# Attention of the first batch by groups of 192 tokens over all heads, in row and column halves of the array

## The chip, the cores and the metric

One Trainium2 chip, one of its cores. The time is microseconds from start to end of one execution on the device, several executions per kernel. Engines are named as in the profile: PE is TensorE's matmuls, PEld its weight loads, DVE VectorE, ACT ScalarE, POOL GpSimd, SP SyncE.

The kernel before has two levels of time, which matter throughout. All its 43 executions, over all experiments, lie either at 314.4 to 316.1 us (15 of them) or at 319.3 to 323.7 (28), with none between. "High level" and "low level" are only names, for times of the kernel before near 320 and near 315 us.

## The reference

Sliding-window attention (batch 8, 8 heads, 576 tokens, head size 64, window 64), then an expert layer on all 4608 tokens.

```python
scores = scale * q @ k.T                      # (8, 8, 576, 576)
mask = (rel >= 0) & (rel < 64)
attn = softmax(where(mask, scores, -1e9))     # divided by sum + 1e-9
x = (attn @ v).transpose(0, 2, 1, 3).reshape(4608, 512)
h = x @ w_in                                  # 512 -> 2048
out = (h * sigmoid(h)) @ w_out                # 2048 -> 512
```

## The kernel before

The kernel describes its work as operations with prices in microseconds, simulates them once when it is built, and emits each engine's instructions in the order that comes out. On the chip that order is fixed; only semaphores say when.

The expert layers run over nine tiles of 512 tokens, first layer (512 to 2048) and then second. TensorE does these products almost without a gap, and the attention of the next batches is woven between them. Nothing can be woven into the start: the first tile needs the attention of batch 0. In the kernel before this goes by pairs of heads, each over all 576 tokens in three groups:

```python
def values(op, n, b, pj, g):                  # per (pair of heads, group of 192 tokens)
    for x in range(3):
        s = 2 * pj * NB + 3 * g + x
        nc.tensor.matmul(at_pv(op)[:, x], lhsT=es[n % NE][:, x].rearrange("p h i -> p (h i)"),
            rhs=vv[b % NK][:, s:s + NB + 1:NB, 0:D + 1], start=(x == 0), stop=(x == 2))
def inverse(op, n):                           # tokens in partitions: 6 sums per partition
    nc.vector.reciprocal(out=rcs[n % NRC], in_=at_pv(op)[:, :, :, D])
# ... the product with the reciprocal, broadcast along the free dimension, as 128x384,
# ... then back_both(): six transposes to features in partitions, and a copy into the bridge
```

The values carry a column of ones, so the 65th column of each output is the sum of exponentials. Tokens lie in partitions, so there are only six sums in each partition: the reciprocal is 128x6. The price is that the output has to be turned for the expert layer.

Two buffers hold the values of two batches; VectorE makes a copy shifted by 64 tokens after each load.

The softmax here doesn't subtract the row's maximum and nothing guards it: scores larger than these inputs give would overflow.

Of the kernel before, what the change touches and what calls it, by code (L numbers as in the profile page):

```python
# [14 lines left out]
class Plan:  # L15
# [12 lines left out]
    def add(self, cls, us, fn, deps=(), lat=0.08, gate=None, dma=None, pool=None, table=None, b=0):  # L28
        if b > 1 and cls in ("cast", "lift", "spread", "mask", "norm"):
            lat = 0.2  # L30
        op = dict(us=us, first=self.rank[cls] + b if b or cls not in self.rank0 else self.rank0[cls], fn=fn, deps=[d for d in deps if d is not None], lat=lat, gate=gate, dma=dma,
                  pool=pool, table=table, seen=None, n=self.count, until=[], bank=None)
        self.count += 1
        self.queues.setdefault(cls, []).append(op)
        return op
# [11 lines left out]
    def run(self):  # L47
# [7 lines left out]
        while left:  # L55
# [6 lines left out]
            while moved:  # L62
                moved = False
                for e in engines:
# [3 lines left out]
                    for c in can[e]:  # L68
# [8 lines left out]
                        if op["pool"] and not any(self.done(self.banks[i]) for i in self.pools[op["pool"]]):  # L77
                            continue
# [4 lines left out]
                    if op["pool"]:  # L83
                        banks = self.banks
                        op["bank"] = min((i for i in self.pools[op["pool"]] if self.done(banks[i])),
                                         key=lambda i: max([u["seen"] for u in banks[i]], default=0.0))
                        banks[op["bank"]] = op["until"]
# [24 lines left out]
def kernel(ctx, tc, q, k, v, w_in, w_out, out):  # L112
    nc = tc.nc
# [15 lines left out]
    PARTS = {0: [(0, 192), (192, TT)]}  # L129
    NXQ, NXK, NXO = 4, 2, 3  # L130
    NRAW, NOX, NRC = 2, 2, 12
    NIV, NPM = 2, 1
# [18 lines left out]
    natbs = [keep.tile([NR, 2 * NM * D], BF16, name=f"natb{i}") for i in range(NNB)]  # L151
# [3 lines left out]
    es = [keep.tile([128, 3, 2, 64], BF16, name=f"e{i}") for i in range(NE)]  # L155
    rcs = [keep.tile([128, 3, 2], FP32, name=f"rc{i}") for i in range(NRC)]
# [5 lines left out]
    bridge = keep.tile([128, B * NB, NDC, 64], BF16, name="bridge")  # L162
# [7 lines left out]
        rank=dict(prime=-8, one=-9, first=-9, dma=-1, ld0=-1, ld1=-1, st=-2, xo=-1.5, xk=-1.4, silu=-3, out=-2, pv=0, ot=0, s=1, moe=99, warm=200, turn=2,  # L170
                  norm=0, inverse=0, bridge=0, exp=1, mask=1, lift=2, spread=2, shift=2, cast=4, late=5, clear=9),
        rank0=dict(turn=-6, cast=-6, lift=-5, shift=-4.5, exp=-4, mask=-4, inverse=-3.5, norm=-3, bridge=-3.2),
        ahead=dict(s=-5.5, exp=-4.6, pv=-5.5, inverse=-4.3, norm=-4.2, ot=-5.5, bridge=-4.25),
# [32 lines left out]
    def clear_vv(i):  # L206
        nc.vector.memset(vv[i][:, :, D:D + 1], 1.0)
        nc.vector.memset(vv[i][0:64, 0, 0:D], 0.0)

    def clear_k(i):  # L210
        nc.vector.memset(kt[i][:, 0:64].bitcast(FP32), 0.0)
# [7 lines left out]

    c_ident = p.add("one", {"POOL": 1.3}, const_ident)  # L220
# [3 lines left out]
    c_q = {i: [p.add("first", {"ACT": 1.0}, lambda e, i=i, hh=hh: clear_q(i, hh), [c_zero]) for hh in range(2)]  # L224
# [7 lines left out]

    def load_cast(w, b, pj, kk):

        nc.gpsimd.dma_start(  # L235
            out=natbs[w].rearrange("p (h y) -> p h y", h=2),
            in_=(q, k)[kk][b, 2 * pj:2 * pj + 2].rearrange("h (p m) d -> p h (m d)", m=NM),
        )

    def load_first(i, kk):  # L240
        nc.sync.dma_start(
            out=nats[i].rearrange("p j m x -> p (j m x)").bitcast(FP32).rearrange("p (h y) -> p h y", h=2),
            in_=(q, k)[kk][0, 0:2].rearrange("h (p m) d -> p h (m d)", m=NM),
        )

    def cast_first(e, i, w):
        copies[e](out=natbs[w], in_=nats[i].rearrange("p j m x -> p (j m x)").bitcast(FP32))

# [44 lines left out]
    def turn_heads(op, w, hs):  # L293

        pst = at_bf16(op).rearrange("x (m p) -> x m p", m=NM)
        heads = natbs[w].rearrange("p (h m d) -> p h m d", h=2, m=NM)
# [57 lines left out]
    def scores_idle(op, b, pj, g):  # L354

        nc.tensor.matmul(
            banks[op["bank"]][:, 0:384], lhsT=ident,
            rhs=(bias0 if g == 0 else bias).rearrange("k x h i -> k (x h i)"), start=True, stop=False)
        for x in range(3):
            t = 3 * g + x  # L360
            nc.tensor.matmul(
                at_sp(op)[:, x], lhsT=kt[b % NK][:, pj * S + t * 64:pj * S + t * 64 + 128],
                rhs=qbd[b % NK][:, pj, :, t * 64:t * 64 + 64], start=False, stop=(x == 2),
            )

# [32 lines left out]
    def ox0(n):  # L398
        return oxs[n // NP % NOX][:, :, n % NP]

# [5 lines left out]
    def normal_both(e, op, n):  # L406

        pv, rc, ob = at_pv(op), rcs[n % NRC], ox0(n)
        if e == "DVE":
            nc.vector.tensor_mul(ob.rearrange("k x (h d) -> k x h d", h=2), pv[:, :, :, 0:D],  # L410
                                 rc.unsqueeze(3).to_broadcast([128, 3, 2, D]))
            return
        for x in range(3):
            nc.scalar.mul(ob[:, x].rearrange("k (h d) -> k h d", h=2), pv[:, x, :, 0:D], rc[:, x, 0:1])

    def back_both(op, n):
        for x in range(3):
            for hh in range(2):
                r = slice(64 * hh, 64 * hh + 64)
                nc.tensor.matmul(banks[op["bank"]][r, 64 * x:64 * x + 64], lhsT=ox0(n)[:, x, r],  # L420
                                 rhs=ident[:, r], start=(x == 0), stop=(x == 2))

    def turn_o(n, b, g):
        n0, i = b * NB + 3 * g, n // NP
# [9 lines left out]
    def to_bridge(e, op, b, pj, g):  # L434
        n0 = b * NB + 3 * g
# [3 lines left out]
    def first_layer(bank, j, ft, c, lo, hi):  # L439
        nc.tensor.matmul(  # L440
            banks[bank["bank"]][:, lo:hi], lhsT=w_in_sb[:, c, ft * 128:(ft + 1) * 128],
            rhs=bridge[:, (j * TT + lo) // 64:(j * TT + hi) // 64, c], start=(c == 0), stop=(c == NDC - 1),
# [26 lines left out]
    exps = {}  # L469

# [13 lines left out]
    def add_batch_qk(b):  # L484
        pool = "at" if b else "all"
        slot, parts = {}, {0: [], 1: []}
        for pj in range(NP):
            kq_done[(b, pj)] = []
            busy = s_last.get((b - NK, pj), []) + ([c_k[b % NK]] if b < NK else [])
            for kk in range(2):  # L490
# [29 lines left out]
                if (b, pj) == (0, 0):  # L520
                    i = n_nat[0] % NN
                    n_nat[0] += 1
                    ld = p.add("ld0", {"SP": 0.45 if kk else 1.2}, lambda _, i=i, kk=kk: load_first(i, kk), dma=1.15)
                    ca = [p.add("cast", {"ACT": 0.84, "DVE": 0.56}, lambda e, i=i, w=w: cast_first(e, i, w), [ld], b=b)]
                    nat_free[i] = ca[0]
                else:
                    ca = [p.add("dma", {"POOL": 0.66}, lambda _, w=w, pj=pj, kk=kk: load_cast(w, b, pj, kk),
                                [natb_free.get(w)], dma=0.55 if b else 0.75)]
# [3 lines left out]
                for hs in ([(0,), (1,)] if b == 0 and not kk else [(0, 1)]):  # L532
                    twos = b > 0 and not kk
# [33 lines left out]

    def add_batch_attention(b):
        pv_last[b], o_rows = [], []
        pool = "at" if b else "all"  # L570
        for g, pj in [(g, pj) for pj in range(NP) for g in range(NG)] if b < NPM else [(g, pj) for g in range(NG) for pj in range(NP)]:
                n = len(g_pv)

                ahead = "0" if b == 0 and g == 0 else ""
                if b == 0:
                    pool = "at" if pj >= 2 and g else "all"
                s = p.add("s" + ahead, {"PE": 0.17 if b else 0.4}, None,
                          kq_done[(b, pj)] + g_pv[n - NE:n - NE + 1] * (n >= NE) + ([] if b else c_bias) + c_q.get(b, []),
                          lat=0.1, gate=scores_may_run, pool=pool, b=b)
                s["fn"] = lambda _, s=s, pj=pj, g=g: (scores if b else scores_idle)(s, b, pj, g)  # L580
                s_last[(b, pj)] = [s]
                ex = p.add("exp" + ahead, {"ACT": 0.5}, lambda _, s=s, n=n: expo(s, n), [s], table="exp", b=b)
                s["until"] = [ex]
                exps.setdefault(b, []).append(ex)
                ma = ex
                if b:
                    ma = p.add("mask", {"DVE": 0.37}, lambda _, n=n, g=g: masking(n, g), [ex, *c_mask], b=b)
                pv = p.add("pv" + ahead, {"PE": 0.17}, None,
# [4 lines left out]
                rc = p.add("inverse" + ahead, {"DVE": 0.21}, lambda _, pv=pv, n=n: inverse(pv, n), [pv] + ([c_ob[n % NOB]] if b else [])  # L593
                           + g_norm[n - NRC:n - NRC + 1] * (n >= NRC), b=b)
                by = {"DVE": 0.37}
                if b >= NXO or (b, g) == (NXO - 1, NG - 1):
                    no = [p.add("norm" + ahead, by, lambda e, pv=pv, n=n, hh=hh: normal_rows(pv, n, hh),
# [4 lines left out]
                    if pj == NP - 1:  # L602
                        xo[n // NP] = [p.add("xo", {"SP": 1.4}, lambda _, n=n, g=g: turn_o(n, b, g), o_rows, dma=1.6)]
# [4 lines left out]
                if b == 0:  # L608
                    no = [p.add("norm" + ahead, {"DVE": 0.56, "ACT": 0.9} if ahead or pj < 2 else {"DVE": 0.56}, lambda e, pv=pv, n=n: normal_both(e, pv, n),
                                [rc] + g_back[n - NP * NOX:n - NP * NOX + 1] * (n >= NP * NOX))] * 2  # L610
                else:
                    no = [p.add("norm" + ahead, by, lambda e, pv=pv, n=n, hh=hh: normal(e, pv, n, hh), [rc], b=b)
                          for hh in range(2)]
                g_norm.append(no[1])
                pv["until"] = no
                ot = p.add("ot" + ahead, {"PE": 0.1 if b else 0.25}, None, no + [c_twoi], lat=0.1, pool=pool, b=b)
# [119 lines left out]
```

## Time and profile before

| | before |
|---|---|
| time, first four runs | 315.95, 319.32, 321.06, 321.66 us |
| span of the profiled run (high level) | 318.8 us |
| first layer starts | 22.1 us |
| second layer starts | 41.9 us |
| longest wait of PE behind a mask | 4.0 us, at 182 us |

The starts are read from the products that use each weight. The columns are line, engine, operation, out<-in, count, then least, median and greatest duration in ns, then the first and last start in microseconds.

```profile
L440 PE MATMUL mp<-bridge,w_in_sb x640: 243/379/382, 22.1 to 301.4; 128*128 128x512 bf16 x128, 128*128 128x192 bf16 x16, 128*128 128x320 bf16 x16
```

Two rows of the groups by form (line, engine, operation, names, shapes, count, then busy us, mean ns of one, then idle time before):

```profile
L381 DVE RECIPROCAL rc<-at 128x6 f32<-128x6 f32 x91 | 17.5, 194 | 10.1 <-PE at L375 8.0 <-ACT ot L455 0.3
...
L410 DVE TENSOR_TENSOR ox<-at,rc 128x384 bf16<-128x384 f32 x6 | 3.2, 541 | 0.1
```

Last, the wait behind a mask that the table names (PE's line, what it waited for, total us, times, longest us):

```profile
PE at L375 <- DVE e L370: 4.0, 1, 4.0
```

### The profile page before, as it was taken

To read this page: it belongs to the slowest core of one execution; us is meant where nothing else is said; L and a number is where in the kernel's file an instruction comes from. 1 tells how busy PE (TensorE), PEld (TensorE's weight loads), DVE (VectorE), ACT (ScalarE), POOL (GpSimd) and SP (SyncE) were. 2 spreads that over 40 slices of the span, in tenths; PEclk is the share of its full clock that TensorE was granted. 3 is DMA by queue.
4 is the path that set the end of the run, shared out by engine and by line. 5 is a ranking of instruction groups with operands and counts; after the bars stand their busy time and mean duration, and the time that the engine had idled before them with its cause. 6 is when DMAs were issued, how large, how long until landed. Compare 5 with 4: busy or idle time off the path is not lost.

```text
span 318.8 us, 6010 instructions
## 1 busy us (share of the span) xinstructions
PE 307.9 (97%) x2198; PEld 168.4 (53%) x2223; DVE 154.5 (48%) x467; ACT 193.4 (61%) x374; POOL 119.2 (37%) x159
## 2 busy tenths in 40 slices
PE   8999999999999999999999869999999999999996
PEld 4778666545664556445544445446544444444444
DVE  4894748934799898923990159606920000000000
ACT  8898786889776565568356721668166126415611
POOL 8947859496829777564454000000000000000000
PEclk9999999999999999999999979999999999999999
DMA  9999999999999999999999933400340020020012
GB/s 144 164 196 186 193 195 161 127 243 129 187 165 135 176 154 152 163 163 163 154 191 175 142 64 90 84 0 36 80 93 2 35 97 0 2 99 33 2 61 70
DMA packets 138108, 37.51 MB, mean 118 GB/s; under 512 B 122464, under 2 KB 133600, under 8 KB 138080
## 3 DMA queue, kind: packets, MB, share of 16 engines
q0 software_dynamic: 95712, 18.06, 74.4%
q1 hardware_dynamic: 42368, 19.08, 33.6%
q8 instruction: 17, 0.28, 0.4%
q14 instruction: 11, 0.09, 0.1%
HBM read 36.70 MB, written 9.44 MB: 145 GB/s over the span
## 4 chain that ended last, share of the span: by engine, by line
PE 85%; DVE 6%; DMA 4%; issue 2%; ACT 1%; POOL 1%; DVEq 0%; POOLq 0%; ACTq 0%
PE mp L449 36%; PE mp L440 32%; PE at L375 5%; PE at L349 4%; DMA vv<-in_v_dram 4%; DVE qbd L314 2%; PE at L680 1%; PE mp L680 1%; DVE ox L404 1%; POOL vv L272 1%; DVE qbd L268 1%; DVE vv L337 1%; DVE vv L335 1%; PE at L308 1%; PE at L420 1%
## 5 line engine op out<-in xcount | busy, mean ns | idle before, releaser
L449 PE MATMUL mp<-w_out_sb,g 128*128 128x512 bf16 (+2 forms) x583 | 141.6, 369 | 1.0
L440 PE MATMUL mp<-bridge,w_in_sb 128*128 128x512 bf16 (+2 forms) x640 | 130.7, 358 | 0.7 <-ACT g L446 0.6
L446 ACT ACTIVATE g<-mp 128x512 bf16<-128x512 f32 (+2 forms) x160 | 86.3, 556 | 29.8 <-PE mp L440 29.3
L440 PEld LDWEIGHTS <-w_in_sb 128*128 128x128 bf16 x640 | 60.1, 98 | 60.3 <-issue 1.4
L449 PEld LDWEIGHTS <-g 128*128 128x128 bf16 x608 | 55.0, 98 | 42.7
L455 ACT COPY ot<-mp 128x512 f32<-128x512 f32 (+2 forms) x34 | 19.0, 561 | 72.1 <-PE mp L449 62.7
L404 DVE TENSOR_TENSOR ox<-at,rc 64x192 bf16<-64x192 f32 x128 | 45.2, 353 | 2.5
L254 POOL DMA_DIRECT2D nat<-in_k_dram x48 | 36.4, 761 | 24.3 <-DMA nat<-in_k_dram 13.0
L367 ACT ACTIVATE e<-at 128x384 bf16<-128x384 f32 x90 | 38.8, 497 | 10.6 <-PE at L349 9.8
L370 DVE TENSOR_TENSOR e<-e,mask 128x384 bf16<-128x384 bf16 x84 | 26.6, 350 | 33.6 <-ACT e L367 32.8
L272 POOL DMA_DIRECT2D vv<-in_v_dram x32 | 32.3, 1014 | 13.1 <-PE at L375 7.2
L375 PE MATMUL at<-vv,e 128*128 128x130 bf16 x273 | 29.8, 220 | 4.1 <-DVE e L370 4.0
L375 PEld LDWEIGHTS <-e 128*128 128x128 bf16 x288 | 22.5, 97 | 20.0 <-DVE e L370 7.6
L254 POOL DMA_DIRECT2D nat<-in_q_dram x32 | 23.4, 735 | 8.1 <-DMA nat<-in_q_dram 4.6
L349 PEld LDWEIGHTS <-kt 128*128 128x128 bf16 x252 | 18.6, 100 | 10.0 <-issue 2.8
L349 PE MATMUL at<-qbd,kt 128*128 128x128 bf16 x252 | 23.6, 222 | 0.3
L381 DVE RECIPROCAL rc<-at 128x6 f32<-128x6 f32 x91 | 17.5, 194 | 10.1 <-PE at L375 8.0
L314 DVE COPY qbd<-at 64x288 bf16<-64x288 bf16 x26 | 12.5, 480 | 11.1 <-ACT qbd L314 7.6
L387 DVE TENSOR_TENSOR ob<-at,rc 64x192 bf16<-64x192 f32 x40 | 14.0, 350 | 0.8
L314 ACT COPY qbd<-at 64x288 bf16<-64x288 bf16 x22 | 10.5, 476 | 2.8 <-DVE qbd L314 2.5
L268 DVE COPY qbd<-raw 64x1152 bf16<-64x1152 bf16 x16 | 8.1, 505 | 8.4 <-DMA raw<-nat 8.0
L235 POOL DMA_DIRECT2D natb<-in_q_dram x15 | 10.0, 665 | 4.9 <-PE at L375 1.4
(69 smaller groups left out, 158.0 us busy)
## 6 DMA issues: line engine op xcount, KB each, us to landing
out_dram<-ot SPq DMA_DIRECT2D x35, 256.0 KB, 2.4
vv<-in_v_dram POOLq DMA_DIRECT2D x32, 144.0 KB, 7.3
nat<-in_k_dram POOLq DMA_DIRECT2D x48, 72.0 KB, 7.9
nat<-in_q_dram POOLq DMA_DIRECT2D x32, 72.0 KB, 7.6
natb<-in_q_dram POOLq DMA_DIRECT2D x15, 144.0 KB, 6.4
w_in_sb<-in_moe_w_in_dram POOLq DMA_DIRECT2D x8, 256.0 KB, 8.7
w_out_sb<-in_moe_w_out_dram POOLq DMA_DIRECT2D x8, 256.0 KB, 7.8
natb<-in_k_dram POOLq DMA_DIRECT2D x7, 144.0 KB, 5.9
```

The source lines that it names most:

```text
L254: nc.gpsimd.dma_start(out=rows(i)[:, pj % 2, :, 64 * hh:64 * hh + 64], in_=(q, k)[kk][b, 2 * pj + hh].rearrange("(m p) d -> p m d", p=NR),)
L272: queue[e].dma_start(out=vv[b % NK][:, 2 * g0 + 1:2 * g1 + 1:2, 0:D], in_=v[b].rearrange("h s d -> (h s) d").rearrange("(g p) d -> p g d", ...
L314: copies[e](out=qbd[b % NK][64 * hh:64 * hh + 64, pj, hh].rearrange("x (p m) -> x p m", m=NM)[:, :, r::2], in_=at_bf16(op)[64 * r:64 * r + ...
L349: nc.tensor.matmul(at_sp(op)[:, x], lhsT=kt[b % NK][:, pj * S + t * 64:pj * S + t * 64 + 128], rhs=qbd[b % NK][:, pj, :, t * 64:t * 64 + 6 ...
L367: nc.scalar.activation(out=es[n % NE], in_=at_sp(op), func=ACTF.Exp, scale=scale)
L370: nc.vector.tensor_mul(es[n % NE], es[n % NE], mask0 if g == 0 else mask)
L375: nc.tensor.matmul(at_pv(op)[:, x], lhsT=es[n % NE][:, x].rearrange("p h i -> p (h i)"), rhs=vv[b % NK][:, s:s + NB + 1:NB, 0:D + 1], star ...
L404: nc.vector.tensor_mul(ox(n)[:, :, r], pv[r, :, hh, 0:D], rc[r, :, hh:hh + 1].to_broadcast([64, 3, 64]))
L440: nc.tensor.matmul(banks[bank["bank"]][:, lo:hi], lhsT=w_in_sb[:, c, ft * 128:(ft + 1) * 128], rhs=bridge[:, (j * TT + lo) // 64:(j * TT + ...
L446: nc.scalar.activation(out=gts[gt][:, lo:hi], in_=banks[bank["bank"]][:, lo:hi], func=ACTF.Silu)
L449: nc.tensor.matmul(banks[bank["bank"]][:, 0:hi - lo], lhsT=gts[gt][:, m * 128:(m + 1) * 128], rhs=w_out_sb[:, f, lo:hi], start=(f == 0), s ...
L455: copies[e](out=ots[ot][:, lo:hi], in_=banks[bank["bank"]][:, 0:hi - lo])
```

## The change

The intent: start the expert layers sooner. Batch 0 is loaded and attended to by groups of 192 tokens over all eight heads. Scores use row halves of the array (head size 64 is the contraction); values and sums use column halves, with v as weights, so that the output comes out with features in partitions and needs no turning. The sums now lie along the free dimension, and matmuls with ones repeat them over 64 partitions. A ring of 48 blocks in place of 72 for the bridge makes room. The first tile is no longer cut into 192 and 320 tokens. The core of the diff:

```diff
-    PARTS = {0: [(0, 192), (192, TT)]}
+    PARTS = {}
+    NBR = 48
...
+    ones = keep.tile([128, 64], BF16, name="ones")
+    sums = [keep.tile([128, 384], FP32, name=f"sum{i}") for i in range(2)]
...
+    for kk in range(2):
+        loads0[(0, kk)] = p.add("start", {"POOL": 0.66}, lambda _, kk=kk: load_group(kk, 0, kk), dma=1.1)
...
+    def values_columns(op, n, c, g):
+        for x in range(3):
+            for j in range(2):
+                for hh in range(2):
+                    nc.tensor.matmul(
+                        at_six(op["bank"])[64 * hh:64 * hh + 64, x, j],
+                        lhsT=vv[0][:, (4 * c + 2 * j + hh) * NB + 3 * g + x, 0:D], rhs=es[n + hh][:, x, j],
+                        start=(x == j == 0), stop=(x == 2 and j == 1))
+        for hh in range(2):
+            nc.tensor.matmul(banks[op["bank2"]][64 * hh:64 * hh + 64, 0:384], lhsT=ones,
+                             rhs=es[n + hh].rearrange("k x h i -> k (x h i)"), start=True, stop=True)
+
+    def inverse_columns(op, n):
+        nc.vector.reciprocal(out=sums[n // 2 % 2], in_=banks[op["bank2"]][:, 0:384])
+
+    def normal_columns(op, n, c, g):
+        nc.vector.tensor_mul(bridge[:, 3 * g:3 * g + 3, 2 * c:2 * c + 2], at_six(op["bank"]),
+                             sums[n // 2 % 2].rearrange("k (x j i) -> k x j i", x=3, j=2))
...
+                rc = p.add("inverse0", {"DVE": 0.53}, lambda _, pv=pv, n=n: inverse_columns(pv, n),
+                           [pv] + (g_norm[n - 4:n - 3] if n >= 4 else []))
```

(The line numbers of the profiles after differ: the first layer is L498, the second L507, the reciprocal L327, its product L330.)

## The prediction

> **What bounds the kernel now.** I read the page's table of engines and its slices first, then busy time by stretch, then the chain of waits, then the rows of single instructions.
>
> ```profile
> PE 307.9 (97%) x2198; PEld 168.4 (53%) x2223; DVE 154.5 (48%) x467; ACT 193.4 (61%) x374; POOL 119.2 (37%) x159
> ...
> PE   8999999999999999999999869999999999999996
> ...
> DMA  9999999999999999999999933400340020020012
> ```
>
> TensorE is busy 97% of the span, and the DMA engines are occupied from about 2 to 184 us. That 97% flatters: before the first expert layer starts, TensorE runs fillers and small matmuls. So I cut the run where the first layer begins, at 22.1 us, and where the second begins, at 41.9 us.
>
> ```profile
> 0.00:22.10 22.10, 20.37 (x267) 13.59 (x268) 15.20 (x53) 19.90 (x39) 18.35 (x31) 1.00 1.34 166
> 22.10:40.00 17.90, 17.30 (x219) 13.13 (x217) 12.00 (x29) 14.46 (x40) 13.50 (x19) 1.00 1.55 190
> ```
>
> The columns are stretch, length, then busy time of PE, PEld, DVE, ACT and POOL, granted clock, DMA share and GB/s. The last counts the bytes as written (bf16): 166 GB/s over 22.1 us is 3.67 MB, while q, k and v of batch 0 are 3 x 4608/8 x 512 x 2 B = 1.77 MB and each of the two weights 2.10 MB. Up to 22.1 us ACT is 90% busy and DVE 69%; in the last six microseconds of it both are over 90%. The front is the attention of batch 0, and everything after it is a queue of matmuls. The first layer waits for all exponentials of batch 0 and for the outputs of the first 192 tokens, so some attention is left over and is woven into it:
>
> ```profile
> 22.28 0.66 PE mp L440 x8
> 22.94 0.21 PE at L420 x6
> 23.16 0.60 PE mp L440 x6
> ...
> 37.77 0.48 ACT qbd L314
> 38.27 0.44 ACT g L446
> 38.71 0.53 ACT kt L327
> 39.24 0.35 ACT g L446
> ```
>
> (Chain of waits: start, length, what.) The L420 pieces are six transposes back of one (pair of heads, group), 0.21 us each. At 38.3 and 39.2 us the chain leaves TensorE: SiLU stands behind the copies of batch 1's q and k on ACT. The other hole that matters lies far from the change:
>
> ```profile
> 171.67 12.93 DMA vv<-in_v_dram
> 184.59 0.03 issue
> ...
> 185.69 0.24 DVE e L370
> 185.94 0.05 issue
> 185.99 0.51 PE at L375 x3
> ```
>
> Batch 7's values need 12.9 us to land. VectorE's fixed order holds their shift ahead of a mask of batch 6, so TensorE sits idle 4.0 us. The stretch 185 to 190 us then has a granted clock of 0.66.
>
> **What the skill says, and whether this trace agrees.** (1) "TensorEngine Tiling (Array Packing)", Theoretical Speedup and Instruction Overhead: a contraction or output width of at most 64 allows up to two tiles at once, but a matmul costs about 60 cycles however few its columns. Before has no row halves to test. Its column halves agree that little is gained at small width: twelve transposes of 96 columns into halves take 0.38 us where six full ones take 0.23 us (the pieces of 0.38 and about 0.23 us in the chain). (2) "VectorE: DVE Perf Modes", Why PSUM operands drop a tier: fp32 from PSUM runs at one element per cycle. The trace agrees: a 128x384 product from PSUM takes 541 ns. (3) "DMA: Bandwidth & Descriptors", Why small descriptors are slow: a fixed cost per piece. The trace agrees: from 4 to 10 us, with v in 256 B reads, 142 GB/s are written; from 40 to 45 us, mostly weights, 206. (4) "TensorE: Matmul & The Clock Gate", What's actually happening: the clock rises after about 3.4 us of activity. The first fillers are about twice as long as later ones, and the clock of 0.66 after the 4.0 us hole agrees too.
>
> **The change, part by part.**
>
> Loads. The first q and k lose the fast path from SP (288 KB as fp32, landed 3.4 to 3.7 us after issue) and their two ACT casts of 0.83 us. Instead, three groups of 192 tokens, all heads, come through GpSimd: 196 KB each of q and k, in 512 B reads where before had 1536 B, and v in 256 B reads as before. Total bytes stay 1.77 MB. At the 142 GB/s of the 4 to 10 us stretch that is 12.5 us. First bytes at about 2.3 us (the first queue in before takes until 1.7 us, and GpSimd spends some 0.8 us on issuing) put the last v at about 14.8, and the last k, which 197 KB of v follow, at 13.4. Completion adds about 1.5 (estimate from v landing at least 3.7 us after the start of an issue of 1.0 us that moves 147 KB). So k of group 2 is usable at about 14.9, v at 16.3.
>
> From k to the last output. Sixteen transposes 0.55. The lift of k, 768 columns: ACT took 0.634 for 576, so 0.83, with the semaphore 0.95. Scores of the first half: two biases 0.16 each, twelve matmuls of 64 columns at no more than 0.04 to 0.05, 0.85 at most, 0.95 with the semaphore. Four exponentials at 0.50 on ACT, 2.0, the second scores hidden beneath them. Values of the second half: twelve small matmuls and two sums of 384 columns, 0.75, with its wait 0.85. Reciprocal 128x384 at one element per cycle, 0.59; product 0.54; semaphores 0.15. Sum 6.6: the first layer may start at 14.9 + 6.6 = 21.5 us, against 22.1. Groups 0 and 1 lie beneath the loads: k of group 1 lands some four microseconds before k of group 2, about what one group costs ACT (four exponentials and its lifts, 3.5 us).
>
> What goes after the start. The first tile is no longer split into 192 and 320 columns. The split pieces ran at about 0.086 us (29 in 2.50) and 0.149 (12 in 1.79), at best about 0.14 for the second: 64 x 0.226 = 14.5 us; 64 of 512 columns at 0.216 are 13.8. Saved 0.7. The leftover L420 groups, six of 0.21, save 1.3; the last leftover values product 0.2. From the first to the second layer before took 19.8 us; after, 13.8 + 2.5 for batch 1's transposes (four times 0.38 + 0.23) + 0.7 for twelve scores = 17.0, plus 0.5 if half of the ACT holes remain. So the second layer starts at 39.0, which would be 2.9 earlier.
>
> But it needs w_out. In the order of issue before the first quarter megabyte of w_out lie 1.77 + 2.10 + 1.77 MB, then 0.26: 1.77 by 14.8 us, the other 4.13 at 187 to 190 GB/s in 22 us, so 37 to 38.5 with completion. That is just early enough. I take 0.4 off for meeting it: 2.5 us.
>
> The ring moves no work: it cuts the bridge from 72 to 48 blocks to make room. Its first wait has batch 5 wait for tile 0, over 50 us old by then. Free.
>
> **The rivals.** *A: the front becomes a wait for DMA.* If 256 B writes of q and k cost like v, 120 GB/s, the loads end 2.3 us later and the first layer starts at about 23.5. The savings after it still stand, so about 318.8. For it: everything now comes through one queue. Against: 512 B reads lie between the two kinds.
> *B: the head start is eaten later.* The DMA engines are full to 184 us, and values of batch 7 set a hole of 4 us. If those loads are bound by DMA and not by released buffers, TensorE merely waits longer: 319. For: GpSimd waits mostly for landings between 142 and 165 us. Against: the chain leads from products of batch 5 through VectorE to the issue of these loads, with 1.1 us of waiting for VectorE last, so it moves along with compute.
> *C: the reordering closes the hole.* All orders are recomputed from estimates, so the shift of v may fall behind the masks: 4.0 + about 1.5 of slow clock off, 311 to 312. Equally a new hole of this kind may open: 321 to 323.
> *D: the first batch stalls inside.* TensorE's order is fixed, so one late load of v holds everything behind it: 2 to 3 us, about 320.
>
> **Range and chances.** 319.3 - 2.5 = 316.8. I lean slightly back for A and B (weight about 0.35 together, 2 us) and slightly forward for C (weight about 0.2, 5 us): 317.0. The three runs of before spread over 5.7 us, which a hole of varying length would explain. The range is 311.5 to 321.5. Faster by over 2% means below 312.9; only C with the whole head start gets there: 0.16. Slower means above 325.7, needing A or D and a new hole: 0.07. The rest, 0.77, is within 2%.
>
> **What would show each step right or wrong.** The first L440-type matmul at 20 to 23.5 us, all exponentials and products of batch 0 before it, and none of the transposes back after it. Last k landing near 15 us, the four last exponentials in a row on ACT, then reciprocal near 0.6 us. The second layer at 39 to 40 us. A DMA rate below 130 GB/s up to 15 us shows A; a longer wait for v of batch 7 with an earlier first layer shows B; none shows C; TensorE idle before values of batch 0 shows D. I am wrong if the first layer starts after 25 us, or if the head start is there at 42 us but not at the end.

## More of the kernel before

The loads of v are another part that matters later.

The load is priced at 1.53 us of transfer a quarter; the shift has a price of its own.

```python
p.add("dma", {"POOL": 1.0}, lambda e, part=part: load_v(e, b, part), busy, dma=1.53)
...
sh = [p.add("shift", {"DVE": 0.1 + 0.18 * (z - a)}, lambda _, hf=hf, a=a, z=z: shift_v(b, hf, a, z), lv[a:z], b=b) for hf in range(2)]
```

## The result, and the profile after

| | before | after |
|---|---|---|
| median | 320.19 us (315.95 to 321.66) | 331.23 us (330.05 to 332.77) |
| span of the profiled run | 318.8 us | 329.9 us |
| first product of the first layer | 22.1 us | 32.5 us, in full flow from 34.96 |
| second layer starts | 41.9 us | 52.0 us |
| wait behind the mask of batch 6 | 4.0 us | 5.3 us |

The change is slower: ratio 1.0438, interval 1.0347 to 1.0528. Below I compare levels and starts, and give ratios only beside them.

The first views of the kernel after, the table of engines and the slices, in the same columns as before:

```profile
PE 308.3 (93%) x2150; PEld 161.3 (49%) x2175; DVE 165.8 (50%) x453; ACT 184.1 (56%) x337; POOL 120.5 (37%) x161
...
PE   5876799999999999999999939999999999999995
...
PEclk9969999999999999999999998999999999999999
```

PE's busy time is the same as before (308.3 against 307.9 us); its share fell. The holes are in the first five of forty slices, and the granted clock dips there. Two stretches of that time:

```profile
22.10:40.00 17.90, 13.25 (x116) 6.06 (x115) 12.39 (x11) 7.24 (x14) 13.55 (x18) 0.89 1.58 190
...
14.00:34.90 20.90, 12.92 (x189) 6.51 (x182) 20.35 (x19) 7.23 (x14) 15.57 (x21) 0.84 1.62 188
```

In the second, from 14.0 to 34.9 us, VectorE (the third number) is busy for 20.35 of 20.90 us with only 19 instructions, while ACT idles for two thirds. More than a microsecond an instruction: a few are very long. The chain of waits names them:

```profile
14.04 2.56 DVE sum L327
...
16.62 0.56 DVE bridge L330
17.18 2.47 DVE sum L327
...
21.44 2.47 DVE sum L327
...
25.46 2.48 DVE sum L327
...
28.63 2.57 DVE sum L327
...
31.22 0.56 DVE bridge L330
31.78 2.47 DVE sum L327
...
34.35 0.57 DVE bridge L330
...
34.96 4.91 PE mp L498 x22
```

All six reciprocals lie on the chain: from 14.04 us on they are 15.0 of 20.9 us, their products 2.3, and the rest is mostly VectorE's shifts of v and a copy of q. The same line's instructions, and the first starts of the layers:

```profile
L327 DVE RECIPROCAL sum<-at x4: 2546/2546/2547, 17.1 to 31.7; 128x384 f32<-128x384 f32 x4
```
```profile
L507 PE MATMUL mp<-w_out_sb,g x25: 377/379/379, 52.0 to 60.0; 128*128 128x512 bf16 x25
```

The reciprocal takes 2.55 us where the prediction had 0.59 and the kernel's own schedule 0.53. Its product, 0.557, is as predicted (0.54). From the full flow of the first layer to the second it is 52.0 - 34.96 = 17.1 us; predicted were 17.5, and before took 19.8. So the savings after the start are there. The start was lost.

The loads of the last group, from GpSimd's timeline (start, length, what, and in brackets the idle time before it and what ended it):

```profile
1.30 0.91 POOL L247 DMA_DIRECT2D natb<-in_q_dram  x1 [0.85 <-POOLq L811]
...
9.88 0.84 POOL L247 DMA_DIRECT2D natb<-in_k_dram  x1
...
17.13 2.23 POOL L368 DMA_DIRECT2D w_in_sb<-in_moe_w_in_dram  x3 [0.27 <-DMA natb<-in_k_dram]
```

The third k is issued at 9.9 us and its transfer ends at 16.9 (GpSimd, which waits for it, goes on at 17.1); predicted were 14.9. This is a second, smaller miss. Last, the wait behind the mask is still there (L448 is that mask):

```profile
PE at L453 <- DVE e L448: 5.3, 1, 5.3
```

### The profile page after: what moved, and what is told of

Its sections match the earlier page's. It is cut to its first block, busy times and chain, and to the rows that moved or that the text cites. A ratio compares the mean times of both kernels' runs of the same rounds, so it can differ in the third digit from the quotient of the medians. Undisturbed runs are those within 1.5% of the kernel's fastest.

```text
span 329.9 us, 5840 instructions
## 1 busy us (share of the span) xinstructions
PE 308.3 (93%) x2150; PEld 161.3 (49%) x2175; DVE 165.8 (50%) x453; ACT 184.1 (56%) x337; POOL 120.5 (37%) x161
## 4 chain that ended last, share of the span: by engine, by line
PE 87%; DVE 6%; DMA 3%; issue 2%; POOL 1%; ACT 0%; DVEq 0%; POOLq 0%; ACTq 0%
PE mp L507 36%; PE mp L498 36%; PE at L453 5%; DVE sum L327 5%; PE at L439 4%; DMA vv<-in_v_dram 3%; PE at L773 1%; PE at L398 1%; PE mp L773 1%; DVE bridge L330 1%; PE at L489 1%; POOL vv L362 0%; DVE vv L289 0%; PE at L389 0%; POOL natb L247 0%
## 5 line engine op out<-in xcount | busy, mean ns | idle before, releaser
L507 PE MATMUL mp<-w_out_sb,g 128*128 128x512 bf16 (+2 forms) x583 | 141.7, 369 | 1.0
L498 PE MATMUL mp<-bridge,w_in_sb 128*128 128x512 bf16 x576 | 130.1, 379 | 1.9 <-DVE bridge L330 1.9
L504 ACT ACTIVATE g<-mp 128x512 bf16<-128x512 f32 x144 | 84.3, 597 | 37.8 <-PE mp L498 37.3
L498 PEld LDWEIGHTS <-w_in_sb 128*128 128x128 bf16 x576 | 55.3, 98 | 64.8 <-issue 2.2
L507 PEld LDWEIGHTS <-g 128*128 128x128 bf16 x608 | 54.8, 98 | 42.1
L445 ACT ACTIVATE e<-at 128x384 bf16<-128x384 f32 x84 | 35.8, 497 | 11.5 <-PE at L439 11.0
L448 DVE TENSOR_TENSOR e<-e,mask 128x384 bf16<-128x384 bf16 x84 | 27.7, 350 | 28.0 <-ACT e L445 26.8
L362 POOL DMA_DIRECT2D vv<-in_v_dram x28 | 28.4, 1019 | 25.7 <-PE at L453 17.4
L453 PE MATMUL at<-vv,e 128*128 128x130 bf16 x252 | 27.5, 220 | 5.4 <-DVE e L448 5.3
L453 PEld LDWEIGHTS <-e 128*128 128x128 bf16 x252 | 20.2, 97 | 21.8 <-DVE e L448 9.9
L404 DVE COPY qbd<-at 64x288 bf16<-64x288 bf16 x23 | 11.0, 480 | 13.6 <-PE at L398 7.0
L404 ACT COPY qbd<-at 64x288 bf16<-64x288 bf16 x25 | 11.9, 476 | 2.3 <-DVE qbd L404 1.9
L773 PE MATMUL at<-ident 128*128 128x384 bf16 x22 | 7.1, 415 | 3.9 <-POOL ident L189 3.6
```

The source lines that it names most:

```text
L362: queue[e].dma_start(out=vv[b % NK][:, 2 * g0 + 1:2 * g1 + 1:2, 0:D], in_=v[b].rearrange("h s d -> (h s) d").rearrange("(g p) d -> p g d", ...
L404: copies[e](out=qbd[b % NK][64 * hh:64 * hh + 64, pj, hh].rearrange("x (p m) -> x p m", m=NM)[:, :, r::2], in_=at_bf16(op)[64 * r:64 * r + ...
L445: nc.scalar.activation(out=es[n % NE], in_=at_sp(op), func=ACTF.Exp, scale=scale)
L448: nc.vector.tensor_mul(es[n % NE], es[n % NE], mask0 if g == 0 else mask)
L498: nc.tensor.matmul(banks[bank["bank"]][:, lo:hi], lhsT=w_in_sb[:, c, ft * 128:(ft + 1) * 128], rhs=bridge[:, j * TB % NBR + lo // 64:j * T ...
L504: nc.scalar.activation(out=gts[gt][:, lo:hi], in_=banks[bank["bank"]][:, lo:hi], func=ACTF.Silu)
```

## The experiments

Three questions: do the six reciprocals set the loss; what are the two levels; and does the restructured front gain anything in itself?

**e1: copies in place of reciprocals.** The result is wrong; nothing else changes, as the schedule's price stays.

```diff
-        nc.vector.reciprocal(out=sums[n // 2 % 2], in_=banks[op["bank2"]][:, 0:384])
+        nc.vector.tensor_copy(out=sums[n // 2 % 2], in_=banks[op["bank2"]][:, 0:384])
```

> The changed kernel with its six 128x384 reciprocals replaced by copies of the same shape (the result is wrong on purpose; no order changes, since the schedule had priced the reciprocal at 0.53 us anyway). Theory R (the reciprocals, 2.55 us each and back to back on VectorE, delay the first layer): the copy takes about 0.55 us, the first layer starts at 23 to 25 us instead of 35.0, the second at 40 to 42 instead of 52, and the time is 317 to 321 us, the ratio to before 0.99 to 1.01. Rival L (loads through one queue land late, and TensorE's fixed order holds up what follows): the first layer still starts after 28 us and the time stays above 325.

Measured: 321.97 us (320.43 to 322.37), all four runs at the level with the wait (4.1 us behind the mask in the profiled one); the ratio is 1.0208 to runs of before that were of the low level. Against high-level runs of before (319.73 to 322.38) it is level. The copy takes 547 ns; the first layer starts at 24.0 us, the second at 41.8:

```profile
L498 PE MATMUL mp<-bridge,w_in_sb x64: 379/379/390, 24.0 to 40.9; 128*128 128x512 bf16 x64
```

Theory R holds, L falls: with the same loads and the same order of everything, taking out the six reciprocals brings the first layer forward by 11 us. But it only brings the kernel back to where it was.

**e2: the true price.** The same instructions, but the schedule knows 2.55 us.

```diff
-                rc = p.add("inverse0", {"DVE": 0.53}, ...
+                rc = p.add("inverse0", {"DVE": 2.55}, ...
```

> The changed kernel scheduled with the reciprocal's measured cost, 2.55 us in place of 0.53; same instructions, other orders. Theory R: VectorE still has 6 x 2.55 us to do after the first sums at 14 us, so the first layer starts at 31 to 35 us and the time is 326 to 332. Rival O (it is the wrong order that costs, not the work): the first layer starts before 28 us and the time falls below 324.

Measured: 325.20 us (324.49 to 326.62), correct, ratio 1.0325. The first layer starts at 33.4 us and the second at 52.0, where after has 32.5 (34.96 in full flow) and 52.0. So the order of the front costs nothing that shows; the work does. The time fell below what I expected of R for another reason: the wait behind the mask is gone from the profile (apart from the wait for GpSimd's constants at the very start, PE's longest are 1.2 and 0.9 us, in the front). A reordering removed it by accident.

**e3: the ring alone,** in the kernel before (48 blocks, and the waits for released tiles).

> The kernel before with the ring for the bridge alone (48 blocks in place of 72, with the waits for released tiles). All theories that lay the loss on the first batch: same as before within 0.7%. Rival W (the ring's waits delay attention of batches 5 to 7): slower by more than 1%, with new waits of copies into the bridge behind first-layer products.

Measured: 314.65, 315.16, 318.92, 319.96 and 323.31 us: the same two levels as before, ratio 0.9993, interval 0.9960 to 1.0026. The ring is free, and it is not what makes the levels. Its profiled run was of the high level and waits 5.3 us behind the mask.

**e4: the reciprocal by itself,** as extra VectorE instructions at the end of the kernel before.

```diff
     p.run()
...
+    for w in (6, 48, 96, 192, 384):
+        nc.vector.reciprocal(out=dst[:, 0:w], in_=src[:, 0:w])       # from SBUF
+    nc.vector.reciprocal(out=dst[0:64], in_=src[0:64])
+    for w in (6, 96, 384):
+        nc.vector.reciprocal(out=dst[:, 0:w], in_=ps[:, 0:w])        # from PSUM
+    nc.vector.tensor_copy(out=dst, in_=ps[:, 0:384])
```

> The kernel before with twelve extra VectorE instructions at its end that measure the reciprocal alone: 6, 48, 96, 192 and 384 columns from SBUF, 384 columns on 64 partitions, 6, 96 and 384 from PSUM, and a copy of 384 from PSUM. Theory R: a fixed cost of about 0.16 us and about 6.2 ns for each column whatever the source and the number of partitions: 0.19, 0.46, 0.75, 1.35 and 2.55 us; 64 partitions also 2.55; the copy about 0.55. Rival P (the reciprocal is slow because its source lies in PSUM): from SBUF 384 columns take 0.6 to 0.8 us.

Measured, in the groups by form:

```profile
L714 DVE RECIPROCAL raw<-at 128x384 f32<-128x384 f32 x1 | 2.6, 2558 | 0.0
L711 DVE RECIPROCAL raw<-raw 128x384 f32<-128x384 f32 x1 | 2.6, 2553 | 0.0
L712 DVE RECIPROCAL raw<-raw 64x384 f32<-64x384 f32 x1 | 2.5, 2545 | 0.0
L711 DVE RECIPROCAL raw<-raw 128x192 f32<-128x192 f32 x1 | 1.4, 1353 | 0.0
...
L711 DVE RECIPROCAL raw<-raw 128x48 f32<-128x48 f32 x1 | 0.5, 454 | 0.0
...
L711 DVE RECIPROCAL raw<-raw 128x6 f32<-128x6 f32 x1 | 0.2, 191 | 0.0
```

From 6 to 384 columns: (2553 - 191) / 378 = 6.25 ns for each column. Half the partitions take the same time, and PSUM costs no more than SBUF, so rival P falls. A copy of 384 columns from PSUM took 0.56 us. The cost goes by columns, not by numbers: repeating the sums over 64 partitions is free for the reciprocal, but laying them out as 384 columns in place of 6 costs 2.4 us each time.

**e5: a correct way around it.** Sums with tokens in partitions again, a 128x6 reciprocal, and TensorE spreads it.

```diff
-            nc.tensor.matmul(banks[op["bank2"]][64 * hh:64 * hh + 64, 0:384], lhsT=ones, rhs=es[n + hh]..., ...)
+        for x in range(3):
+            for hh in range(2):
+                nc.tensor.matmul(banks[op["bank2"]][:, 2 * x + hh:2 * x + hh + 1],
+                                 lhsT=es[n + hh][:, x].rearrange("k j i -> k (j i)"), rhs=ones[:, 0:1], ...)
...
+            nc.vector.reciprocal(out=rcb[n // 2 % 2], in_=banks[op["bank2"]][:, 0:6]...)     # 128x6
+    def spread_columns(op, n):
+        for hh in range(2):
+            for x in range(3):
+                nc.tensor.matmul(banks[op["bank"]][64 * hh:64 * hh + 64, 128 * x:128 * x + 128],
+                                 lhsT=rcb[n // 2 % 2][:, x, hh:hh + 1].to_broadcast([128, 64]), rhs=ident, ...)
+    # ACT copies that to sums; the product stays as it was
```

> The changed kernel with a correct way around the wide reciprocal: sums come out with tokens in partitions (six matmuls of one column), the reciprocal is 128x6, six matmuls against the identity spread it over 64 partitions and ACT copies that to SBUF for the same product. Theory R: the reciprocals take about 0.2 us each, the first layer starts at 24 to 25.5 us, the second at 41.5 to 43, and the time is 319 to 323 us where batch 6 waits behind the values of batch 7, 314 to 318 where it does not. Rival L (late loads and order of the front): first layer after 28 us, time above 325.

Measured: 319.58, 322.73, 323.78 and 324.58 us, correct, ratio 1.0094. The reciprocals take 0.18 to 0.20 us. The first layer starts at 26.0 and the second at 44.1, 0.5 and 1.1 us above the upper ends of what I expected. These times still contain waits behind the mask (1.8 us in the profiled, fastest run). Without them, in e9 and e7 below, the small reciprocal recovers 324.67 - 317.75 = 6.9 us of the 9.25 by which e9 is behind e6. The result is correct, but the added spreading and copying stand in the chain and it does not pass the kernel before.

**e6: the two levels of the kernel before.** One price is changed: the last batch's loads of v.

```diff
-            ... load_v(e, b, part), busy, dma=1.53)
+            ... load_v(e, b, part), busy, dma=3.0 if b == B - 1 else 1.53)
```

> The kernel before with only the price of batch 7's four loads of values in its schedule raised from 1.53 to 3.0 us, so that VectorE's order puts their shift later; no instruction is added or removed. Theory H (the two levels of the kernel before, near 315 and near 320.5, are the wait of batch 6's mask behind that shift, there in some runs and not in others): all runs at 313.5 to 317, and TensorE never waits over 1 us for a mask. Rival: the two levels stay, or the wait moves and costs the same.

Measured: 314.94, 315.05, 315.79 and 316.10 us, correct; the unchanged kernel beside it ran at 315.57, 315.84 and five times at 319.47 to 322.80. The ratio, 0.9889, is to a mixture of its levels. The wait is not there; these are the longest of PE:

```profile
PE at L680 <- POOL ident L181: 1.4, 1, 1.4
PE at L420 <- DVE ox L410: 0.5, 1, 0.5
PE mp L440 <- ACT g L446: 0.4, 2, 0.3
PE at L375 <- ACT e L367: 0.3, 1, 0.3
```

Theory H holds: without the wait the high level is gone. By this the low level of before is its time without the wait, the high one with it, and the order that a price of 1.53 us gives is a race that is lost in 28 of 43 runs. Two limits: no low-level run of the unchanged kernel was profiled, and the new price also reordered some of VectorE's other work from 181 us on. The granted clock is not what makes the levels, since high-level runs at a clock of 1.0 are on record too (319.47 and 319.73 us). This version has no added instruction, and at 315.42 us it is at the low level in every run.

**e7: e5 and e6 together.**

> The small reciprocals of the run before the last together with the higher price of batch 7's loads. Theories R and H together: first layer at 24 to 25.5 us, no wait for a mask, all runs at 314 to 318 us, within 1% of the kernel before where that has no wait; so the restructured front gains nothing in itself. If grouping by tokens gains as predicted (2.5 us), 312 to 313.

Measured: 317.75 us (317.29 to 317.90), correct, no wait for a mask, first layer at 26.4 (later than expected) and second at 44.3. The time is within the expected range, 2.3 us above e6.

**e8: e7, with the first tile as 384 and 128 columns** (so that it needs only two groups at first), **and the first two loads of v ahead of GpSimd's constants.**

> Small reciprocals, the higher price for batch 7, the first two loads of values issued ahead of GpSimd's constants, and the first tile in 384 and 128 columns, so that it needs only two groups at first. First layer at 19.5 to 22 us, second at 38.5 to 40.5, time 311.5 to 314.5. Rival S (the second layer is set by the arrival of w_out and by batch 1's loads, not by the front): first layer as early, but the second starts at 41 us or later or TensorE waits for w_out, and the time is 314 to 317.

Measured: 315.29 us (315.15 to 315.57), correct: level with e6 (315.42). The first layer starts at 21.8 us as hoped, but the second only at 42.1, and PE waits 1.3 us for q of batch 1 in between. That is what rival S said. What moving the two loads ahead brought by itself cannot be told, as the tile was split in the same run: the last k landed at 15.4 us in place of e7's 15.9, and the queue ran dry all the same, a little later.

**e9: the changed kernel without the wait** (the price of e6 alone).

> The changed kernel with only the higher price for batch 7's loads of values in its schedule. Theories R and H: its wait for a mask (5.3 us) goes, the first layer still starts at 35 us, and all runs lie at 324.5 to 327: 9.5 to 11 above the kernel before with the same price (315.4). Rival: the slow front lets the loads run ahead in any case, so the wait was something else and the time stays at 330 to 332.

Measured: 324.67 us (324.48 to 324.90), correct, ratio 1.0221, second layer at 52.1. Together with e10 this is the clean comparison, free of levels.

**e10 and e13: copies in place of reciprocals, without the wait.** The same program twice.

> Copies in place of reciprocals (wrong result on purpose) with the higher price for batch 7. Theories R and H: first layer near 24 us, second near 42, no wait for a mask, all runs at 314.5 to 316.5: level with the kernel before at the same price. Had the front gained the predicted 2.5 us once the reciprocal costs what was assumed, 312.5 to 313.5.

> The run e10 once more, as the partner of the next run on the same chip. As there: first layer near 23 us, second near 42 to 42.5, TensorE waits about 1 us for q of batch 1, time 314.3 to 316.

Measured: 314.86 us (314.31 to 315.92) and 315.07 (314.85 to 315.97), ratio 0.9990 in the second, whose runs of before were mostly of the low level. So the six reciprocals cost 324.67 - 314.86 = 9.8 us, and the front with copies in their place is level with before at its best: 0.4 to 0.6 us below e6 in another call, which is within the spread of these runs, and in e13's own call the interval of the ratio is 0.9966 to 1.0015. The first layer started at 23.0 and 23.9, the second at 42.5 and 42.2.

**e11: e8 with the last three loads of w_in behind the first loads of batch 1.**

> The kernel of the run e8 with the last three loads of w_in moved behind the first loads of batch 1. Theory S (between first and second layer TensorE waits for batch 1's loads, which w_in stands ahead of): the 1.3 us of waiting for q of batch 1 go, the second layer starts at 40.5 to 41.3 instead of 42.1, and the time is 313.8 to 314.8. Rival (w_in itself is then late, or w_out): the second layer stays at 42 or later and the time at 315 or more, with waits of TensorE for w_in.

Measured: 315.16 us (314.75 to 316.11), correct; second layer at 41.8, PE still waits 1.0 us for q of batch 1. Neither what S nor what its rival expected: a tie with e8.

**e12: e10 without batch 1's loads of v** (zeroes instead, wrong).

> The run e10 (copies for reciprocals, higher price for batch 7) without the four loads of batch 1's values, which are set to zero in their place (wrong result on purpose); 0.59 MB less in the queue ahead of batch 1's last q and k and of w_out. Theory S (in the chain of e10 and e11 it is DMA from 10.6 to 36.9 us, so the loads set the start of the second layer): the wait of TensorE for q of batch 1 (1.1 us) goes, the second layer starts at 40 to 41 us instead of 42.5, the time falls to 312 to 313.5. Rival E (work on TensorE, ACT and VectorE between first and second layer sets it): the second layer stays at 42 to 42.7, the time at 314.3 to 316.

Measured: 318.65 us (318.39 to 319.30), first layer at 24.6, second at 43.3. A miss on both sides: taking four operations out of the schedule changed all orders, the front started later, and PE lost 3 us between 60 and 140 us. It tells nothing about S or E.

**e14: e13 with one ninth of batch 1's rows of v loaded;** the same instructions in the same order, fewer bytes (wrong).

```diff
-        g0, g1 = part * 9, part * 9 + 9
+        g0, g1 = part * 9, part * 9 + (1 if b == 1 else 9)
```

> The same kernel in the same order of instructions, but the four loads of batch 1's values fetch one ninth of their rows each (the rest is zero from a memset while VectorE is idle; wrong result on purpose): 0.52 MB less in the queue, nothing else moved. Theory S (the loads set the start of the second layer): no wait of TensorE for q of batch 1, second layer 17.5 to 18 us after the first, at 40.5 to 41.3 where the first starts at 23, and the time 1 to 2 us below its partner. Rival E (work between first and second layer sets it): second layer within 0.4 us of its partner, the time too.

Measured: 314.68 us (314.16 to 315.54) beside 315.07. The first starts of the two layers, e13 and then e14:

```profile
L507 PE MATMUL mp<-w_out_sb,g x59: 377/379/381, 42.2 to 60.0; 128*128 128x512 bf16 x59
L498 PE MATMUL mp<-bridge,w_in_sb x64: 379/379/390, 23.9 to 41.3; 128*128 128x512 bf16 x64
```
```profile
L509 PE MATMUL mp<-w_out_sb,g x58: 377/379/382, 42.2 to 60.0; 128*128 128x512 bf16 x58
L500 PE MATMUL mp<-bridge,w_in_sb x64: 379/379/390, 24.2 to 41.3; 128*128 128x512 bf16 x64
```

The wait for q of batch 1 (0.3 us in e13) goes, and the second layer does not move. The first layer started 0.3 us later in e14, so only the wait itself was saved, 18.3 against 18.0 us between the layers. For a first layer that starts at 24 us this fits rival E: 18 us of products, transposes and scores set the second layer. But there were only 0.3 us to find, so S is not refuted for the longer waits. Where the first layer starts earlier, PE waits for q of batch 1: 1.1 us with a start at 23.0 (e10), 1.3 at 21.8 (e8), 0.3 at 23.9 (e13). That these waits are why e8's earlier start brings nothing is what the chain suggests, not what a run has shown; e8 also splits the tile and weaves the last group into it.

## Why the prediction was wrong

By its own steps:

1. *Reciprocal 128x384 "at one element per cycle, 0.59".* This is the step that failed. It measured 2.55 us. The prediction took the rate of a product from PSUM (a row with 384 columns) and applied it to another operation whose only row had six columns. Six times 2.55 - 0.59 is 11.8 us of VectorE; on the path it cost 9.8 us (e9 against e10). In the prediction's sum of 6.6 us from the last k to the first layer only one reciprocal stood; at 2.55 us each, the others no longer fit beneath the loads either, as VectorE's 97% from 14.0 to 34.9 us show.
2. *Groups 0 and 1 "lie beneath the loads".* Right for ACT, with which it was checked; wrong for VectorE, which was not checked: per half group a reciprocal and a product are 3.1 us, 18.6 in all.
3. *Last k at 14.9 us.* It landed at 16.9, and at 15.7 to 16.1 in the four profiles with copies (e1, e10, e13, e14): 0.8 to 2.0 us late. GpSimd's first load began at 1.30 us, not at the 0.74 at which before issued its first, and from 2 to 16 us 130 GB/s were written, not 142, with dips to 37 and 55 GB/s about three to four microseconds after GpSimd's pause for constants (2.95 to 4.26 us). In e8, where that pause comes later, there is one deeper dip (19 GB/s at 7.3 us) in place of the two, which suggests the pause as their cause. From issue to landing k took 7.0 us. Rival A had 2.3 us for slower loads: somewhat more than came. Its cause, that these writes cost like v's, was not tested.
4. *6.6 us from k to the first layer.* With the reciprocal made as cheap as assumed it is 24.0 - 16.0 = 8.0 in e1, 8.2 and 8.3 in e13 and e14, and 6.9 in e10. In e1 k, landed at 16.0, waited 1.1 us for its turn on PE, whose fixed order has other transposes first; from there it is 6.9. So the sum of durations was about right, but the sum has no term for that wait (0.3 us in e10, 1.4 and 1.3 in e13 and e14).
5. *17.5 us from first to second layer.* 17.1 in the kernel after, 17.8 in e1, 18.3 in e13, 18.0 in e14: about right. It is 19.5 in e10, of which 1.1 is PE's wait for q of batch 1. The prediction had w_out as the load to watch; PE waited for q instead.
6. *The gain of 2.5 us.* With the dear reciprocal and the wait out of the way, none is shown (e13 beside before: ratio 0.9990, interval to 1.0015). The first layer was to start at 21.5 and starts at 23.0 to 24.2 in the four profiles with copies, no sooner than the 22.1 and 23.2 of the kernel before and e6. The second layer, which has the savings after the start in it, comes at 41.8 to 42.5 against 41.9 and 42.9. Why the first layer is some 2 us late there was not tested. The late k of point 3 is not it in e1, for no load lies on e1's chain between 3.6 us and the first layer. That chain begins so:

   ```profile
   3.62 1.46 PE at L773 x4
   ...
   7.64 0.32 PE mp L773
   7.96 0.78 PE mp L271 x16
   ```

   L773 are fillers, matmuls that only keep PE busy; L271 are the transposes of the first q. Two loads now go ahead of GpSimd's constant, so PE's first filler waits for it until 3.6 us (1.4 in the kernel before). Thirteen fillers priced at 0.17 us then took 0.32 us or more each, 4.3 us in all, while q and k of the first group had landed at 5.1 and 6.2. In e10 they ended 0.5 us sooner and the first layer starts 1.0 sooner. This fits, but no run left the fillers out.
7. *The ring is free.* Shown by e3.
8. *Rivals B and C, the hole behind the mask.* The hole exists and is worth 6.6 us in the kernel after (331.23 against 324.67), about 5 in the one before. It did not close by itself and moved along with the front, as the prediction's argument against B said: 5.3 us of waiting at 191 us. The guess that the spread of before comes from it is right (e6). Rival D (a late load of v stalls the values) is not what happened: the one wait before values, 1.9 us, was for VectorE's shift of v, which stood behind a reciprocal; with copies (e1) there is 0.7 us in its place, for ACT.

Some of its readings were off as well, without bearing on the result. The piece of 0.23 us that it set against twelve half-width transposes is of the same half-width kind (L420); six full ones (L308) take 0.26 to 0.27 us. The chain shows four leftover L420 groups after 22.1 us, not six. VectorE is 88% busy in the last six microseconds before the first layer, not over 90%. The 142 and 206 GB/s that it sets against each other come from stretches that differ in more than the size of the pieces, so they don't show what a piece costs. The question it left open, whether row halves run two at once, the profile after answers: they start within 0.01 us. And what came, slower by over 2%, had a chance of 0.07, for rivals that did not cause it.

None of the four rivals asked what a new form of instruction costs. All were about transfers and orders, since those had bounded the kernel before; the reciprocal entered as a known quantity. The kernel's own price of 0.53 us pointed the same way, but it was an estimate as well.

## What to carry to other kernels

A duration may be taken from a row of the same operation, not from one of the same shape; where that row has only a few columns, its cost per column is unknown and should be the widest term of the range, or be measured first. A layout that turns sums from partitions into columns multiplies the columns of what VectorE does to the sums (here a reciprocal of 384 in place of 6), so look for the operation that is dear per column before choosing it. And where an order is fixed at build time, two levels of time in one kernel are worth looking into first: here one price, with no new instruction, was worth about 5 us in the runs that lost the race, and the restructuring showed no gain even with cheap copies for its reciprocals.

## What the Trainium skill lacked or had wrong

- "VectorE: DVE Perf Modes", First, the fixed hardware budget, says that the reciprocal is an iterative divide with a repeat count of 8, which should have been a warning; the prediction did not draw on it. Neither that passage nor the page's table of costs gives a time for it. The runs: 191 ns for 128x6, 2553 for 128x384, 6.25 ns for each column, by estimate 6.0 cycles at the page's clock of 0.96 GHz; the same from SBUF and PSUM and for 64 partitions.
- "DMA: Bandwidth & Descriptors", Anatomy of one DMA, gives about 2.0 us of fixed cost and the bytes for one load through GpSimd. It has no figure for several in the queue: the third k, 192 KB, took 7.0 us from issue to landing (5.4 to 7.0 over the profiles of this front), with loads of v and q issued 0.8 to 2.5 us before it still under way.
